# A branch hint ahead of the last branch, and loads moved from SyncE's queue to GpSimd's, in an attention and MLP kernel

## The chip, the cores and the metric

The kernel runs on one core of one Trainium2 chip. The metric is the device time of one execution in microseconds, the median of several runs. A profiled execution also gives a span, which is the time from the first to the last instruction of the program. Engines are named as in the profile: PE (TensorE matmul; PEld its weight loads), DVE (VectorE), ACT (ScalarE), POOL (GpSimd) and SP (SyncE). A q behind a name means the engine's sequencer, which handles waits, branches, register moves and DMA issues.

## What is computed

Eight batches of 12 heads, 448 positions and 64 channels go through attention with normalised queries and keys, and the result through a layer norm and a two-layer MLP with a residual:

```python
q_n, k_n = rmsnorm(q, g_q), rmsnorm(k, g_k)
scores = (q_n @ k_n.T) / sqrt(64)
attn = softmax(scores)                       # per head
x = heads_to_columns(attn @ v)               # 8 x 448 x 768
xn = (x - mean(x)) / sqrt(var(x) + 1e-6) * g_ln
out = x + maximum(xn @ w_ch1, 0) @ w_ch2     # 768 -> 3072 -> 768
```

## The kernel before, in words

The program has two ways to compute this. The **fast path** (class `_Fast`) works with 16-bit matmuls and a softmax without a maximum, which holds only while some sums and scales stay in bounds. The **general path** (`_general`, L786 to L894) is a slow loop over the eight batches that computes everything again and is safe for any data. The fast path always runs; while it runs it counts on DVE whether all its numbers were in bounds, and writes a flag (`flag`, L757, called from `run_rest` at L739). At the end each engine loads the flag into a register (L935) and branches on it (L936): into the general path if the flag is set, past it if not. For the inputs here it is not set, so the general path is only jumped over. In the stream of instructions of each engine it stands between the branch and the end of the program, so its length is the length of the jump.

Behind the branch, on the way past the general path, each engine raises the semaphore counts that the general path would have raised (these instructions carry the branch's line, L936). Then comes the end of the program (these carry L963): SP waits, one after another, until all DMA counters and all engines have reached their final counts, then two barriers over all engines follow, with a reset of the semaphores between them. The program also begins with a barrier over all engines (L952), which POOL gathers and releases.

Work of the fast path is cut into 25 **units** (`UNITS`, L23), each of one or two pairs of heads of one batch. `load_unit` (L168) brings a unit's k, q and v, for each of them a main part over 128 partitions (`load_main`, L125) and a rest in two halves (`load_left`, L131). Units up to 10 are loaded on SP's queue, later ones on POOL's (L171). Unit tiles come from a pool of two buffers, so unit 10's load goes into the buffer that unit 8 had. `pieces` (L189) prepares a unit: squares and sums for the norm, k times the two gains (`kg`, L225, on POOL at L229), the split of k into high and low halves, q scaled (L68), copies of v (L285, L291), and transposes by DMA on SP (L258 to L271) for later units. The order of work on PE, ACT, POOL and SP is written out by hand: by the list `ORDER` for the start, then by `attention` (L487), which gives each step of a unit a place among the scores and values of earlier pairs, and by `run_rest` (L729), which lays these steps between chunks of the MLP of the batch before. On DVE the scheduler sets the order.

`run_rest` walks over the batches. The last batch has no attention beside it any more: its MLP chunks (`mlp_chunks`, L641) run alone, 24 of the first layer (L652) and then those of the second (L668); DVE adds the residual (L672), and `store` (L704) issues the output on SP (L709) and, for the last 64 rows, on SP and ACT (L712). The normalised input of each MLP is transposed by DMA on SP (L624).

SP's and ACT's DMAs take eight semaphores in turn as counters, POOL's eight others.

The general path before has its 36 loads (L799) and its store (L893) on SP; each needs an address that depends on the loop's counter, which uses registers of the issuing engine.

Of the kernel before, what the change touches and what calls it, by code (L numbers as in the profile page):

```python
# [14 lines left out]
ENG = mybir.EngineType  # L15
# [61 lines left out]
class _Fast:  # L77
# [88 lines left out]
                                 for x in t]  # L166

    def load_unit(self, u):  # L168
        b, hs, m = UNITS[u]
        t = self.p_in.tile([128, 3, 14, D], FP32, tag="qkv", name="qkv")  # L170
        eng = self.nc.sync if u < 11 else self.nc.gpsimd  # L171
        for n in (1, 0, 2):
            self.load_main(eng, n, t[:, n, 0:6 * m], b, hs, 2 * m)
            self.load_left(eng, n, t[:, n, 6 * m:7 * m], b, hs, 2 * m)
        self.loads[u] = [t[:, n] for n in range(3)]

# [539 lines left out]
    def upto(self, target):  # L716
        while self.pos < min(target, len(self.steps)):
            for call in self.steps[self.pos]:
                call()
            self.pos += 1  # L720
# [8 lines left out]
    def run_rest(self):  # L729
        steps, mark, upto = self.steps, self.mark, self.upto  # L730
        tail = 13
        for b in range(B):
            chunks = list(self.mlp_chunks(b))
            total = sum(c for c, _ in chunks)
            if b + 1 == B:
                for i, (_, emit) in enumerate(chunks):
                    emit()
                    if i == 2:
                        self.flag()  # L739
                break  # L740
            start, goal = self.pos, mark[b + 1]
            done, items = 0.0, None
            for i, (cost, emit) in enumerate(chunks):
                if items and len(chunks) - i <= len(items):
                    items.pop(0)()
                emit()
                done += cost
                upto(int(min(goal, start + (goal - start) * done / (total - 960 * tail))))
                if self.pos >= goal and items is None:
                    items = self.ln_list(b + 1)  # L750
                    items.pop(0)()
            for op in items:
                op()
            if b + 2 == B:
                upto(len(steps))
# [30 lines left out]
def _general(tc, sh, q, k, v, g_q, g_k, out):  # L786

    nc = tc.nc
    P1, NS = 112, 4
    with ExitStack() as ctx:  # L790
# [4 lines left out]
        with tc.For_i(0, B) as b:  # L795
            for h in range(H):
                qkv = sb.tile([P1, 3, NS, D], FP32, tag="qkv", name="qkv")
                for n, src in enumerate((q, k, v)):
                    nc.sync.dma_start(  # L799
                        qkv[:, n].rearrange("p s d -> p (s d)"),  # L800
                        src[bass.ds(b, 1), h].rearrange("o (p s) d -> p (o s d)", p=P1))
                sq = sb.tile([P1, 2, NS, D], FP32, tag="sq", name="sq")
# [7 lines left out]
                for e in range(2):  # L810
# [3 lines left out]
                    out=kg, in0=qkv[:, 1],  # L814
# [70 lines left out]
            for s in range(NS):  # L885
                for g in range(2):
                    pC = ps.tile([P1, 384], FP32, tag="pC", name="pC")
                    for f in range(NFF):
# [1 line left out]
                                         start=(f == 0), stop=(f == NFF - 1))  # L890
                    nc.vector.tensor_tensor(out=x[:, s, ts(g, 384)], in0=pC,
                                            in1=x[:, s, ts(g, 384)], op=ALU.add)
            nc.sync.dma_start(out[bass.ds(b, 1)].rearrange("o (p s) d -> p (o s d)", p=P1),  # L893
                              x.rearrange("p s d -> p (s d)"))  # L894


@with_exitstack
def kernel(
    ctx: ExitStack,
    tc: tile.TileContext,  # L900
    q: bass.AP,
    k: bass.AP,
    v: bass.AP,
    g_q: bass.AP,
    g_k: bass.AP,
    moe_g_ln: bass.AP,
    moe_w_ch1: bass.AP,
    moe_w_ch2: bass.AP,
    out: bass.AP,
):  # L910
    nc = tc.nc
    sh = _Shared()
    const = ctx.enter_context(tc.tile_pool(name="const", bufs=1))
    sh.id16 = const.tile([128, 128], FP16, name="id16")
    make_identity(nc, sh.id16)
    sh.ones = const.tile([128, 1], FP32, name="ones")
    nc.vector.memset(sh.ones, 1.0)
    sh.warm = const.tile([128, 1], FP32, name="warm")
    sh.w2 = const.tile([128, NFF, DM], FP16, name="w2")
    sh.gg = sh.w2[:, 0, 0:4 * D].bitcast(FP32).rearrange("p (n d) -> p n d", n=2)  # L920
    sh.gprod = const.tile([128, D], FP32, name="gprod")
    sh.gmax = const.tile([128, 1], FP32, name="gmax")
    sh.gln = const.tile([128, DM], FP32, name="gln")
    sh.flag = const.tile([1, 1], INT32, name="flag")
    sh.w1 = const.tile([128, NDC, FF], FP16, name="w1")

    with ExitStack() as fctx:
        manual = {ENG.PE, ENG.Activation, ENG.Pool, ENG.SP}
        with tc.manual_schedule(engines=manual | {ENG.DVE}):
            fast = _Fast(fctx, tc, sh, q, k, v, (g_q, g_k), moe_g_ln, moe_w_ch1, moe_w_ch2, out)  # L930
            fast.run_first()
        with tc.manual_schedule(engines=manual):
            fast.run_rest()

    val = nc.values_load(sh.flag[0:1, 0:1], min_val=0, max_val=1)  # L935
    with tc.If(val > 0):  # L936
        _general(tc, sh, q, k, v, g_q, g_k, out)


# [28 lines left out]
```

## Time and profile before

| what | value |
|---|---|
| time before, median of 3 runs | 607.65 us |
| lowest and highest run | 606.86 and 607.78 us |
| time of the profiled execution | 606.57 us |
| its span | 604.8 us |
| PE busy in the span | 575.8 us (95%) |
| DVE, ACT, POOL busy | 287.3, 358.4, 184.0 us |

A row of the profile that stands for one line reads: line, engine, operation, tile, count, then durations in ns (least, median, most), then the starts of the first and of the last in microseconds of the span. A row of the timeline begins with start and length in microseconds; what stands in brackets is the idle time before it and what ended it. "DMA to landing" is the time from a transfer's issue to its count on its semaphore. The page's DMA queues give the packets, the megabytes and a share of time; the queues of kind "instruction" carry the program's own code.

### The profile page before, as it was taken

The numbers are of one execution on the slowest core, as the hardware profiler recorded it, in microseconds if no ns is written. First come the engines' busy times: TensorE is split into PE (matmuls) and PEld (weight loads), VectorE is DVE, ScalarE is ACT, GpSimd is POOL, SyncE is SP. The second block draws the span as 40 slices with busy tenths as digits, with TensorE's granted clock in tenths as the row PEclk, the third lists the DMA queues.
The fourth block names the chain that finished last, engine by engine and source line by source line (L and its number), as shares of the span: only waits on it lengthen the run. The fifth ranks groups of instructions, "written<-read, shape, count | busy, mean of one in ns | idle before, by whom it ended". The sixth has DMA issues, their size and how long they took to land.

```text
span 604.8 us, 11485 instructions
## 1 busy us (share of the span) xinstructions
PE 575.8 (95%) x4500; PEld 340.3 (56%) x4500; DVE 287.3 (48%) x643; ACT 358.4 (59%) x673; POOL 184.0 (30%) x245
## 2 busy tenths in 40 slices
PE   2887999999999999999999999999999999999995
PEld 1555666655565666654566666654566666654564
DVE  5899567734356256714256255734256322530011
ACT  5996887368843697448754498538755387124200
POOL 2853432233541355332542345424412000000000
PEclk9999999999999999999999999999999999999999
DMA  8998999484966487948856486948724330130011
GB/s 229 272 198 198 218 226 190 94 175 122 150 140 133 106 111 158 179 123 97 130 140 125 96 118 156 191 114 124 140 58 84 79 62 1 37 95 0 1 53 57
DMA packets 130861, 75.29 MB, mean 124 GB/s; under 512 B 96656, under 2 KB 121040, under 8 KB 130800
## 3 DMA queue, kind: packets, MB, share of 16 engines
q1 hardware_dynamic: 114048, 45.12, 38.4%
q0 software_dynamic: 16080, 28.94, 22.5%
q8 instruction: 37, 0.61, 0.4%
q10 hardware_dynamic: 672, 0.43, 0.2%
q14 instruction: 24, 0.20, 0.1%
HBM read 52.36 MB, written 11.01 MB: 105 GB/s over the span
## 4 chain that ended last, share of the span: by engine, by line
PE 88%; ACT 2%; DVE 2%; issue 0%; DVEq 0%
PE psC L668 36%; PE psH L652 35%; PE psS L353 8%; PE oA L408 5%; PE oB L410 2%; PE psS L359 1%; ACT E L371 1%; PE tr L316 0%; ACT khl L215 0%; PE psU L698 0%; DVE stat L576 0%; ACT hT L654 0%; PE tr L330 0%; DVE xn L597 0%; DVE x L425 0%
## 5 line engine op out<-in xcount | busy, mean ns | idle before, releaser
L652 PE MATMUL psH<-xnT,w 128*128 128x512 f16 (+1 forms) x1134 | 242.0, 353 | 0.0
L668 PE MATMUL psC<-w,hT 128*128 128x384 f16 (+1 forms) x1368 | 234.8, 323 | 0.0
L371 ACT ACTIVATE E<-psS,rr_all 128x448 f16<-128x448 f32 x312 | 193.4, 635 | 48.7 <-PE psS L353 47.8
L654 ACT ACTIVATE hT<-psH 128x512 f16<-128x512 f32 (+1 forms) x189 | 104.0, 550 | 132.2 <-PE psH L652 130.9
L668 PEld LDWEIGHTS <-hT 128*128 128x128 f16 x1368 | 127.2, 98 | 78.8 <-issue 4.3
L652 PEld LDWEIGHTS <-w 128*128 128x128 f16 x1134 | 102.4, 98 | 83.3 <-issue 2.9
L353 PE MATMUL psS<-qU,kU 128*128 128x448 f16 x288 | 101.0, 357 | 8.6 <-ACT E L371 5.7
L408 PEld LDWEIGHTS <-E 128*128 128x128 f16 x936 | 64.5, 98 | 44.5 <-issue 5.1
L229 POOL TENSOR_TENSOR qkv<-qkv,gprod 128x896 f32<-128x896 f32 x21 | 43.6, 2078 | 92.5 <-ACT khl L215 41.1
L408 PE MATMUL oA<-v,E 128*128 128x65 f16 x864 | 66.6, 194 | 0.1
L672 DVE SCALAR_TENSOR_TENSOR x<-psC,rs_all,x 128x384 f32<-128x384 f32 x48 | 29.2, 616 | 78.5 <-PE psC L668 78.1
L128 POOL DMA_DIRECT2D qkv<-in_k_dram x14 | 11.2, 796 | 137.7 <-ACT E L371 82.5
L410 PE MATMUL oB<-v,E 128*128 128x65 f16 x288 | 51.9, 194 | 0.1
L423 DVE RECIPROCAL rec_all<-oA 128x6 f32<-128x6 f32 x48 | 9.3, 194 | 88.1 <-PE oA L408 87.6
L218 DVE TENSOR_REDUCE ssq<-khl 128x14 f32<-128x896 f32 (+1 forms) x24 | 25.6, 1065 | 44.6 <-ACT khl L215 44.5
L353 PEld LDWEIGHTS <-kU 128*128 128x128 f16 x288 | 28.1, 98 | 25.7 <-issue 5.8
L218 DVE TENSOR_REDUCE ssq<-qn 128x14 f32<-128x896 f32 (+1 forms) x25 | 26.1, 1046 | 21.9 <-ACT qn L215 21.8
L68 DVE SCALAR_TENSOR_TENSOR qn<-qkv,rr_all 128x256 f16<-128x256 f32 (+1 forms) x72 | 26.4, 425 | 18.1 <-ACT rr_all L222 18.1
L410 PEld LDWEIGHTS <-E 128*128 128x128 f16 x312 | 30.2, 97 | 0.2 <-DVE xl L430 0.2
L425 DVE TENSOR_TENSOR x<-oA,rec_all 128x384 f32<-128x384 f32 x48 | 26.8, 558 | 1.5
L576 DVE BATCH_NORM_STATS2 stat<-x 128x6 f32<-128x256 f32 (+1 forms) x75 | 26.0, 404 | 0.6
L240 DVE TENSOR_TENSOR khl<-qkv,khl 128x896 f16<-128x896 f32 x21 | 22.7, 1079 | 4.0 <-ACT khl L237 3.9
(111 smaller groups left out, 443.1 us busy)
## 6 DMA issues: line engine op xcount, KB each, us to landing
out_dram<-x SPq DMA_DIRECT2D x20, 384.0 KB, 2.5
qkv<-in_k_dram POOLq DMA_DIRECT2D x14, 384.0 KB, 3.8
qkv<-in_q_dram POOLq DMA_DIRECT2D x14, 384.0 KB, 5.5
qkv<-in_v_dram POOLq DMA_DIRECT2D x14, 384.0 KB, 7.2
w<-in_moe_w_ch_dram POOLq DMA_DIRECT2D x3, 1536.0 KB, 13.0
w<-in_moe_w_ch_dram POOLq DMA_DIRECT2D x2, 2304.0 KB, 22.8
qkv<-in_k_dram SPq DMA_DIRECT2D x7, 384.0 KB, 6.1
qkv<-in_q_dram SPq DMA_DIRECT2D x7, 384.0 KB, 5.7
```

What stands on the lines that cost most here:

```text
L68: nc.vector.scalar_tensor_tensor(out=out, in0=x, scalar=8.0, in1=r.unsqueeze(2).broadcast_to([x.shape[0], g, D]), op0=ALU.mult, op1=ALU.mult)
L218: nc.vector.tensor_reduce(out=c["ssq"][:, n], in_=c["sq", n], axis=AX.X, op=ALU.add)
L229: (nc.vector if u in DVE_KG else nc.gpsimd).tensor_tensor(out=c["t"][1], in0=c["t"][1], in1=sh.gprod.unsqueeze(1).broadcast_to([128, g, D] ...
L353: nc.tensor.matmul(ps[0][:, 0:S], c["main"][:, ts(i, 128)], c["q"][:, ts(h, S)], start=True, stop=True)
L371: nc.scalar.activation(out=o, in_=x[:, 0:S], func=AFT.Exp, scale=self.units[u][3][:, g:g + 1], bias=EXP_BIAS)
L408: nc.tensor.matmul(oA[:, t, cs], E[:, ts(t, 128)], rhs, start=(i == 0 and t == 0), stop=(i == 6 and t == 2))
L410: nc.tensor.matmul(oB[:, cs], E[:, 320:448], rhs, start=(i == 0), stop=(i == 6))
L425: nc.vector.tensor_tensor(out=x[:, :, 128 * hp:128 * hp + 128].rearrange("p t (e d) -> p t e d", e=2), in0=oA[:, :, :, 0:D], in1=rec[:, 0: ...
L652: nc.tensor.matmul(ps[:, 0:N], sh.w1[:, dc, ts(f, 128)], xnT[:, dc, 0:N], start=(dc == 0), stop=(dc == NDC - 1))
L654: nc.scalar.activation(out=hT[:, f, 0:N], in_=ps[:, 0:N], func=AFT.Relu)
L668: nc.tensor.matmul(ps[:, 0:g[1]], hT[:, f, ts(t, 128)], sh.w2[:, f, cols], start=(f == 0), stop=(f == NFF - 1))
L672: nc.vector.scalar_tensor_tensor(out=x[:, cols], in0=ps[:, 0:g[1]], scalar=self.rs[:, b, t:t + 1], in1=x[:, cols], op0=ALU.mult, op1=ALU.add)
```

## The change

There are three edits. The branch gets the label "general", and `run_rest` marks, 40 chunks ahead of the end of the last batch's MLP, a place for a hint on all five engines that this branch is likely taken. The general path's loads and its store are issued by POOL in place of SP. And of unit 10's six DMA groups one, the main part of v, is issued by POOL in place of SP.

```diff
     def load_unit(self, u):
+        nc = self.nc
         b, hs, m = UNITS[u]
         t = self.p_in.tile([128, 3, 14, D], FP32, tag="qkv", name="qkv")
         eng = self.nc.sync if u < 11 else self.nc.gpsimd
         for n in (1, 0, 2):
-            self.load_main(eng, n, t[:, n, 0:6 * m], b, hs, 2 * m)
+            self.load_main(nc.gpsimd if u == 10 and n == 2 else eng, n, t[:, n, 0:6 * m], b, hs, 2 * m)
             self.load_left(eng, n, t[:, n, 6 * m:7 * m], b, hs, 2 * m)
...
             if b + 1 == B:
                 for i, (_, emit) in enumerate(chunks):
+                    if i == len(chunks) - 40:
+                        self.tc.mark_branch_hint_location("general", "LikelyTaken", [ENG.PE, ENG.DVE, ENG.SP, ENG.Activation, ENG.Pool])
                     emit()
...
                 for n, src in enumerate((q, k, v)):
-                    nc.sync.dma_start(
+                    nc.gpsimd.dma_start(
                         qkv[:, n].rearrange("p s d -> p (s d)"),
...
-            nc.sync.dma_start(out[bass.ds(b, 1)].rearrange("o (p s) d -> p (o s d)", p=P1),
+            nc.gpsimd.dma_start(out[bass.ds(b, 1)].rearrange("o (p s) d -> p (o s d)", p=P1),
                               x.rearrange("p s d -> p (s d)"))
...
-    with tc.If(val > 0):
+    with tc.If(val > 0, label="general"):
         _general(tc, sh, q, k, v, g_q, g_k, out)
```

The edits add three lines, so lines of the changed kernel behind them are numbered one to three higher: the branch is L939 there, the reading of the flag L938, the end of the program L966.

## The prediction

> **What bounds the kernel now.** I read the page first (shares and the 40 slices), then the waits of TensorE, then the chain that ended last, then, line by line, the last eight microseconds.
>
> ```profile
> span 604.8 us, 11485 instructions
> PE 575.8 (95%) x4500; PEld 340.3 (56%) x4500; DVE 287.3 (48%) x643; ACT 358.4 (59%) x673; POOL 184.0 (30%) x245
> PE   2887999999999999999999999999999999999995
> ```
> TensorE is busy in nearly every slice but the first five (some 75 us) and the last. Its waits from 80 us on are one row:
>
> ```profile
> PE psS L353 <- ACT E L371: 0.4, 2, 0.2
> ```
> So from 80 us on nothing outside TensorE makes time or loses it, until its last matmul. The chain from 590 us shows where that is:
>
> ```profile
> 589.90 8.52 PE psC L668 x76
> 598.43 0.02 issue
> 598.45 0.42 DVE xl L672
> ```
> Compute ends at 598.9 us, and the span at 604.8: 5.9 us in which no engine computes. Those are the stage of this change. The views of L712 (the last stores, from 598.5 us), L935 (each engine reads the flag), L936 (the branch, and what stands first behind it) and L963 (the closing waits and barriers) show it; the times are first and last starts.
>
> ```profile
> L712 SPq DMA_DIRECT2D out_dram<-xl x1: 466/466/466, 598.9 to 598.9; - x1
> L712 ACTq DMA_DIRECT2D out_dram<-xl x1: 498/498/498, 598.9 to 598.9; - x1
> DMA to landing us min/median/max: 2.2/2.7/3.1
> ```
> ```profile
> L935 PEldq TENSOR_LOAD <-flag x1: 488/488/488, 596.8 to 596.8; - x1
> L935 DVEq TENSOR_LOAD <-flag x1: 539/539/539, 598.5 to 598.5; - x1
> L935 ACTq TENSOR_LOAD <-flag x1: 959/959/959, 599.4 to 599.4; - x1
> ```
> ```profile
> L936 SPq EVENT_SEMAPHORE  x8: 17/17/17, 602.6 to 603.1; - x8
> L936 POOLq COMPARE_BRANCH  x1: 53/53/53, 540.6 to 540.6; - x1
> L936 PEldq COMPARE_BRANCH  x1: 4102/4102/4102, 597.4 to 597.4; - x1
> L936 DVEq COMPARE_BRANCH  x1: 72/72/72, 599.1 to 599.1; - x1
> L936 SPq COMPARE_BRANCH  x1: 58/58/58, 599.4 to 599.4; - x1
> L936 ACTq COMPARE_BRANCH  x1: 54/54/54, 600.5 to 600.5; - x1
> L936 ACTq EVENT_SEMAPHORE  x1: 17/17/17, 601.0 to 601.0; - x1
> L936 PEldq EVENT_SEMAPHORE  x1: 51/51/51, 601.5 to 601.5; - x1
> L936 DVEq EVENT_SEMAPHORE  x1: 21/21/21, 602.4 to 602.4; - x1
> ```
> ```profile
> L963 SPq EVENT_SEMAPHORE  x12: 27/28/28, 603.2 to 603.8; - x12
> ```
> Read it engine by engine. From branch to next instruction SP takes 3.2 us (599.4 to 602.6), DVE 3.3 (599.1 to 602.4), PE 4.1 inside the branch's own record, ACT 0.5 (600.5 to 601.0). DVE, PE and ACT wait there for nothing but their own finished work. So on three engines the branch itself stalls. The page's instruction queues say with what:
>
> ```profile
> q8 instruction: 37, 0.61, 0.4%
> q14 instruction: 24, 0.20, 0.1%
> ```
> Code is loaded in pieces, 0.61 MB in 37 packets (16 KB) and 0.20 MB in 24 (8 KB). In the built program the general path lies between branch and end: 156 instructions on SP, 438 on DVE, 1809 on PE, 141 on ACT, 26 on POOL. The one that jumps 141 pays 0.5 us, those that jump 156 and more pay over 3: the target's code isn't there and has to be fetched.
>
> SP sets the end. Once its code is there it passes 20 waits in a row, 8 of L936 and 12 of L963, 602.6 to 603.8, none of them held up (0.06 to 0.07 us each, their spacing); from the start of the last one to the end of the span it is 1.0 us (603.8 to 604.8: drains, two barriers).
>
> **The change, part by part.** General path: 36 loads and a store go from SP's code to POOL's. By the built programs SP then jumps 37 instructions, POOL 139; and the 8 waits of L936 leave SP, POOL getting 4 and one count-up instead. DVE, PE and ACT jump as far as before. For SP the new jump is shorter than ACT's, which paid 0.5 us, and longer than POOL's 26, so I price it at ACT's 0.5: SP's first closing wait starts at 599.9 in place of 603.2. POOL's longer jump, even if it stalled 3.3 us like DVE's, is at 540.6 us, and POOL is needed again only in the closing barriers, behind SP's last wait: 60 us of cover. With less cover than 3.3 us it would cost the difference.
>
> What is late next? SP's 12 waits must see, in program order, the DMA lanes and then DVE's, PE's and ACT's work past their branches. With SP alone mended, DVE is last (602.4): SP passes its count in the tenth wait and two more behind it, the twelfth starting at 602.6. Before it started at 603.8. That is worth 1.2 us.
>
> The hint: the built program has a branch hint on all five engines. It stands not 40 chunks from the end but as the first instruction on PE, DVE, ACT and SP and ahead of the first of POOL's kernel instructions, some 600 us before the branch, with no other branch in between. Which way is "taken"? The trace says that the way past the general path is the one that costs a far jump, so that is the one that a hint can help. No row shows a hint's work, so it is bounded: nothing (DVE and PE stall as before), or the whole stall down to ACT's 0.5 us (DVE at 599.6, PE at 597.9). I take the second: a hint names its branch, the code of the end has to come in only once, and both engines stand near the branch long before it (PE's last 76 matmuls alone take 8.5 us, twice its stall, and DVE follows them).
>
> [...]
>
> With SP, DVE and PE free, ACT (601.0) and the last two stores remain. The stores are issued at 598.9; over the whole run L712 reads:
>
> ```profile
> DMA to landing us min/median/max: 1.9/2.2/3.1
> ```
> At the median they have landed at 601.1 (bounds: the least here and the most of the last pair, 600.8 and 602.0). DMAs of SP and ACT take eight counters in turn, and there are now 296 of them in place of 297: the last two stores hold the last two counters that SP looks at, and one wait or none lies behind. So the twelfth starts at 601.2 in place of 603.8. Gain: **2.6 us**, with bounds 1.7 and 2.8.
>
> Costs at the start. The register moves for the general path's addresses go from SP to POOL, ahead of POOL's drain, for which all engines wait at 0.5 us:
>
> ```profile
> L952 SPq MOVE  x4: 29/34/42, 0.0 to 0.2; - x4
> L952 POOLq EVENT_SEMAPHORE  x2: 17/17/17, 0.5 to 0.6; - x2
> L952 SPq DRAIN  x1: 7/7/7, 0.3 to 0.3; - x1
> ```
> SP was ready at 0.3 and not the last, so its relief is worth nothing; four moves spaced 0.06 make POOL, which was last, 0.2 us later. A hint costs each engine what a short sequencer instruction does, 0.02 (the waits) to 0.07 (the branches): 0.1 at most, on all engines beside each other. TensorE waits in its first slices, so both go through to the end: **0.3 us**, bounds 0 and 0.4.
>
> Unit 10: the load of v, 128 partitions, goes from SP to POOL. On POOL it stands behind unit 9's L229 and ahead of its casts:
>
> ```profile
> 99.15 1.29 DVE L68 SCALAR_TENSOR_TENSOR qn<-qkv,rr_all 128x256 f16<-128x256 f32 x4
> 108.61 2.08 POOL L229 TENSOR_TENSOR qkv<-qkv,gprod 128x896 f32<-128x896 f32 x1 [12.78 <-DMA qU<-qn]
> 110.64 0.83 POOL L285 CAST v<-qkv 128x768 f16<-128x768 f32 x1
> 111.40 0.64 POOL L291 CAST vl<-qkv 64x128 f16<-64x128 f32 x2
> 130.15 0.80 POOL L128 DMA_DIRECT2D qkv<-in_k_dram  x1 [18.11 <-ACT E L371]
> L128 POOL DMA_DIRECT2D qkv<-in_v_dram x14: 782/784/792, 134.1 to 430.6; - x14
> 127.52 0.60 SPq L128 DMA_DIRECT2D qkv<-in_v_dram  x1
> 129.52 2.15 SPq L258 DMA_TRANSPOSE kU<-khl  x1
> L624 SPq DMA_TRANSPOSE xnT<-xn x4: 1215/1234/1237, 113.6 to 117.6; - x4
> DMA to landing us min/median/max: 2.7/2.8/2.8
> L652 PE MATMUL psH<-xnT,w x12: 379/379/379, 122.4 to 124.9; 128*128 128x512 f16 x12
> ```
> It waits for unit 8's last reader on DVE (the first row, done at 100.4), so it issues at 110.7 and takes 0.78; the casts come 0.8 later, and POOL then has 18.1 us of idle time to take that up. SP's transposes of unit 9 come up to 0.6 earlier. The transfer moves from 127.5 to 110.7, and may meet the four xnT transposes, the last issued at 117.6 and landed 2.8 us later (the row under theirs) at 120.4; TensorE wants xnT at 122.4. Cover 2.0 us, past that one for one. With TensorE never waiting there: **0**, bounds 0 and 1.
>
> **Sum.** 2.6 - 0.3 = 2.3 us. The profiled execution took 606.57 us, 1.77 outside its span; it would take 604.3, with a span of 602.5. It lies 1.08 below the median of the runs, and since none of the terms scales with that, I take the 2.3 from the median: 607.65 - 2.3 = **605.35 us**.
>
> **Rivals.**
> [...]
> *PE alone pays*: its next instruction at 601.5 goes through SP's last two waits; the twelfth starts at 601.6, gain 2.2 - 0.3 = 1.9: 605.75.
> [...]
>
> **How the numbers follow.** Forecast 0.62, PE alone 0.08, not heeded 0.18, not heeded and SP stalling 0.04, slower 0.08. About 0.2% (1.2 us) is what a measurement of this kernel can tell from no change. Faster by more (under 606.4): 0.62 + 0.08 = 0.70. Within: 0.18 + 0.04 = 0.22. Slower: 0.08. The range takes in the forecast's bounds (1.7 - 0.4 to 2.8 - 0, so 604.85 to 606.35), some way below for the spread of the three runs (606.86 to 607.78), and above up to the unheeded hint: 604.4 to 606.9.
>
> **What would show it.** In the changed kernel's profile: DVE's and PE's L939 instruction behind the branch within 0.5 us (forecast) or over 3 (not heeded); SP's closing waits starting at about 599.9 and one of the last two ending at a landing; a start 0.2 to 0.3 us later; POOL with a 0.78 us load at about 111 and TensorE without new waits behind 80 us. I am wrong if TensorE's last matmul moves by over half a microsecond, if DVE's stall stays, or if the landing slips towards 602.

## The result, and the profile after

The changed kernel takes **604.52 us** (median of 7 runs, 604.02 to 605.83) against 607.65 us (606.86 to 607.84). The ratio is 0.9961 with a 95% interval of 0.9951 to 0.997, that is 2.4 us less (1.8 to 3.0). The profiled execution took 604.02 us with a span of 602.5 us.

From its page first the span, the busy times and TensorE's row of the 40 slices:

```profile
span 602.5 us, 11487 instructions
PE 575.8 (96%) x4500; PEld 340.0 (56%) x4500; DVE 287.3 (48%) x643; ACT 358.5 (60%) x673; POOL 184.8 (31%) x246
PE   2787999999999999999999999999999999999997
```
And the row of TensorE's waits on ScalarE's exponentials, from 80 us on:

```profile
PE psS L354 <- ACT E L372: 0.4, 2, 0.2
```
TensorE does the same work and waits as little. The last slice of its row has gone from 5 to 7: the same tail end of matmuls stands in a shorter remainder. The chain from 588 us says where compute ends now:

```profile
587.96 10.80 PE psC L669 x90
598.76 0.02 issue
598.79 0.42 DVE xl L673
```
That is 599.2 us, 0.3 later than before. From there to the end of the span it is 3.3 us, where it was 5.9 (604.8 - 598.9). This stretch, from DVE's last operation to the end, is called the tail below. The whole gain is in it. The branch's line, in the view that showed it before (the columns are again durations in ns and first and last start in us):

```profile
L939 POOLq COMPARE_BRANCH  x1: 63/63/63, 541.0 to 541.0; - x1
L939 PEldq COMPARE_BRANCH  x1: 393/393/393, 597.7 to 597.7; - x1
L939 PEldq EVENT_SEMAPHORE  x1: 51/51/51, 598.8 to 598.8; - x1
L939 DVEq COMPARE_BRANCH  x1: 84/84/84, 599.4 to 599.4; - x1
L939 SPq COMPARE_BRANCH  x1: 78/78/78, 599.7 to 599.7; - x1
L939 DVEq EVENT_SEMAPHORE  x1: 21/21/21, 600.0 to 600.0; - x1
L939 ACTq COMPARE_BRANCH  x1: 72/72/72, 600.8 to 600.8; - x1
L939 ACTq EVENT_SEMAPHORE  x1: 17/17/17, 601.3 to 601.3; - x1
```
DVE goes from its branch to the next instruction in 0.6 us (it was 3.3). PE's branch takes 0.39 us (it was 4.10), and its next instruction, which waits for PE's last matmul, follows at 598.8, when that is done (587.96 + 10.80 in the chain). SP's own view, the closing waits, is next (twelve of them; the thirteenth instruction, of 17 ns at 601.8, belongs to the barrier behind them):

```profile
L966 SPq EVENT_SEMAPHORE  x13: 17/28/328, 600.0 to 601.8; - x13
```
The same view cut to what starts from 600.95 us on:

```profile
L966 SPq EVENT_SEMAPHORE  x2: 28/28/28, 601.5 to 601.5; - x2
```
And the issues of the last two stores, with the time from issue to landing of the stores there:

```profile
L713 SPq DMA_DIRECT2D out_dram<-xl x1: 466/466/466, 599.2 to 599.2; - x1
L713 ACTq DMA_DIRECT2D out_dram<-xl x1: 498/498/498, 599.2 to 599.2; - x1
...
DMA to landing us min/median/max: 2.0/2.1/2.2
```
SP starts its closing waits at 600.0 instead of 603.2. Ten of the twelve are through by 600.95 (one of them holds SP for 328 ns); the last two both start at 601.5, which is when the later of the last two stores (ACT's, 2.2 us to landing; SP's took 2.0), issued at 599.2, has landed. So a store's landing now ends the kernel, where before it was SP's late arrival at a list of waits that were all met. It does so by little: the last wait also needs ACT, which is past its branch only at 601.3, so an earlier landing would have gained no more than about 0.1 us.

The start: three rows of the program's first microsecond, from the views of L955 (the first barrier) and L966 (the hints carry the line of the program's end), then the load of unit 10 in GpSimd's timeline (start and duration in us). Both stand where they were forecast:

```profile
L955 POOLq MOVE  x4: 29/29/39, 0.2 to 0.4; - x4
L955 POOLq EVENT_SEMAPHORE  x2: 17/17/17, 0.8 to 0.8; - x2
L966 SPq BRANCH_PREFETCH_HINT  x1: 56/56/56, 1.0 to 1.0; - x1
```
```profile
109.28 2.08 POOL L230 TENSOR_TENSOR qkv<-qkv,gprod 128x896 f32<-128x896 f32 x1 [13.13 <-DMA qU<-qn]
111.30 0.80 POOL L128 DMA_DIRECT2D qkv<-in_v_dram  x1
112.10 0.84 POOL L286 CAST v<-qkv 128x768 f16<-128x768 f32 x1
```
The first barrier is gathered at 0.8 instead of 0.5 us. The four hints other than SP's took 50 to 60 ns each.

### The profile page after: what moved, and what is told of

Its sections match the earlier page's. It is cut to its first block, busy times and chain, and to the rows that moved or that the text cites. A ratio compares the mean times of both kernels' runs of the same rounds, so it can differ in the third digit from the quotient of the medians.

```text
span 602.5 us, 11487 instructions
## 1 busy us (share of the span) xinstructions
PE 575.8 (96%) x4500; PEld 340.0 (56%) x4500; DVE 287.3 (48%) x643; ACT 358.5 (60%) x673; POOL 184.8 (31%) x246
## 4 chain that ended last, share of the span: by engine, by line
PE 86%; DVE 3%; ACT 2%; DMA 1%; issue 1%; SPq 0%; DVEq 0%; ACTq 0%
PE psH L653 35%; PE psC L669 34%; PE psS L354 7%; PE oA L409 5%; PE oB L411 2%; PE psS L360 1%; DMA kU<-khl 1%; ACT E L372 1%; DVE stat L577 1%; ACT khl L216 1%; PE psU L699 0%; DVE x L426 0%; DVE ssq L219 0%; ACT hT L655 0%; DVE khl L241 0%
```

## The experiments

The theory to be tested, inferred from the gaps of 3.2 to 4.1 us behind the branches before: a jump to code that isn't at hand stalls an engine for its fetch; the queue moves make SP's jump short; the hint brings DVE's and PE's target in ahead; SP's last closing wait sets the end, whichever engine or store it is that holds it. The rivals are that the moves alone do it, or that one part of the hint alone does.

The profiles' spans can't be set beside each other as they are: compute ended anywhere from 598.9 to 600.7 us in them. So the tail is read from each, and the time from the ratios. Each tail is a difference of two rounded times and good to about 0.1 us. Each ratio is to the kernel before on the same chip; runs 1 to 4 shared a chip, and so did runs 5 to 8.

| run | jumps past the general path | span - end of DVE = tail, us | ratio (95%) |
|---|---|---|---|
| before | SP, DVE, PE stall | 604.8 - 598.9 = 5.9 | 1 |
| whole change | none stalls | 602.5 - 599.2 = 3.3 | 0.9961 (0.9951 to 0.997) |
| 1 moves alone | DVE, PE stall | 604.4 - 599.6 = 4.8 | 0.9977 (0.9968 to 0.9985) |
| 2 hint alone | none stalls | 603.8 - 599.6 = 4.2 | 0.9979 (0.9971 to 0.9988) |
| 3 hint on PE and DVE, no moves | SP stalls | 605.6 - 599.6 = 6.0 | 1.0003 (0.9994 to 1.0012) |
| 4 moves, hint on DVE | PE stalls | 603.7 - 600.3 = 3.4 | 0.9968 (0.9955 to 0.9981) |
| 5 moves, hint on PE | DVE stalls | 605.6 - 600.7 = 4.9 | 0.9984 (0.9973 to 0.9994) |
| 6 moves, hint on PE and DVE | none stalls | 602.8 - 599.2 = 3.6 | 0.9966 (0.9952 to 0.9979) |
| 7 whole change but unit 10 | none stalls | 604.1 - 600.7 = 3.4 | 0.9963 (0.995 to 0.9977) |
| 8 whole change again | none stalls | 603.3 - 600.0 = 3.3 | 0.9963 (0.9951 to 0.9974) |

### 1: the moves alone

```diff
-                    if i == len(chunks) - 40:
-                        self.tc.mark_branch_hint_location("general", "LikelyTaken", [ENG.PE, ENG.DVE, ENG.SP, ENG.Activation, ENG.Pool])
```


> The queue moves alone, no hint on any engine. Theory (a jump to code that is not at hand stalls for its fetch; the moves shorten SP's jump, the hint brings DVE's and PE's target in ahead; SP's last closing wait sets the end): SP passes its branch within 0.5 us, DVE still takes 3.3 us and PE 4.1, DVE is last at about 602.7 of the span, gain 0.9 us, ratio to before 0.9985. Rival (the moves do it all and the hint is decoration): ratio 0.996, DVE and PE through their branches in under 1 us. Start 0.2 us later than before, as with the whole change, by both.

Measured: 605.63 us against 607.13, tail 4.8. Its branch line and SP's closing waits:

```profile
L937 PEldq COMPARE_BRANCH  x1: 4322/4322/4322, 598.1 to 598.1; - x1
L937 DVEq COMPARE_BRANCH  x1: 72/72/72, 599.8 to 599.8; - x1
L937 SPq COMPARE_BRANCH  x1: 58/58/58, 600.2 to 600.2; - x1
L937 DVEq EVENT_SEMAPHORE  x1: 21/21/21, 603.3 to 603.3; - x1
```
```profile
L964 SPq EVENT_SEMAPHORE  x12: 28/28/2048, 600.4 to 603.4; - x12
```
SP is through its jump in 0.2 us, without any hint. DVE takes 3.5 us and PE 4.3, and one of SP's waits holds it for 2.05 us, until DVE is there. The tail is 1.1 us shorter than before; less 0.2 at the start that is the 0.9 expected, at the edge of what the ratio allows (0.9 to 1.9 us). The rival that the moves do it all falls by the two stalls: they are still there.

### 2: the hint alone

The kernel before, with the label and the mark of the hint:

```diff
+                    if i == len(chunks) - 40:
+                        self.tc.mark_branch_hint_location("general", "LikelyTaken", [ENG.PE, ENG.DVE, ENG.SP, ENG.Activation, ENG.Pool])
...
-    with tc.If(val > 0):
+    with tc.If(val > 0, label="general"):
```


> The hint on all five engines alone; loads and stores stay on SP. Theory: SP, DVE and PE all pass their branches within 0.6 us though SP still jumps over 156 instructions; but SP has its 8 + 12 waits, the first held by a store that lands at about 601.2, so that its last wait starts at about 602.4 in place of 603.8: gain 1.4 us less 0.1 for the hints, 1.3, ratio 0.9978. No 0.2 us at the start. Rival (the moves do it all): SP still 3.2 us behind its branch, ratio 1.000.

Measured: 605.92 us against 607.13, tail 4.2. SP in its two stretches of waits:

```profile
L938 SPq EVENT_SEMAPHORE  x8: 17/17/17, 601.5 to 602.1; - x8
L938 SPq COMPARE_BRANCH  x1: 78/78/78, 600.1 to 600.1; - x1
```
```profile
L965 SPq EVENT_SEMAPHORE  x12: 28/28/28, 602.1 to 602.8; - x12
```
With the hint SP's gap is shorter as well, over the 156 instructions that the prediction counted: its next instruction starts 1.4 us behind the branch (3.2 before). That is also 1.9 us behind the issue of SP's own last store at 599.6, for whose landing it was expected to wait (SP's last store took 2.0 us with the whole change), so how much of the 1.4 us is the jump doesn't show. But 8 + 12 waits are still to come, and they take the 1.3 us from 601.5 to 602.8. The tail is 1.7 us shorter, less 0.1 for the hints 1.6; the ratio says 1.3 (0.7 to 1.8). So hint and moves are each worth something by themselves, and both shorten SP's gap (3.2 us before) to 1.4 and 0.2. By the tails they are worth a little less together (2.6 us) than their sum (1.1 + 1.7); by the ratios (2.4 against 1.4 + 1.3, each good to about half a microsecond) that can't be told.

### 3: the hint on PE and DVE, without the moves

As run 2, with `[ENG.PE, ENG.DVE]` as the engines of the hint.

> The hint on PE and DVE alone; loads and stores stay on SP, and SP has no hint. Theory: DVE and PE pass in 0.6 us, but SP stalls 3.2 us and then has its 20 waits, all met: the end stays where it was, ratio 1.000 (0.9995 to 1.0005). Rival (PE's and DVE's stalls set the end, SP only waits for them): gain of 1 to 2 us, ratio 0.997 to 0.998.

Measured: 607.35 us against 607.13, tail 6.0.

```profile
L938 SPq EVENT_SEMAPHORE  x8: 17/17/17, 603.4 to 603.9; - x8
L938 PEldq COMPARE_BRANCH  x1: 393/393/393, 598.1 to 598.1; - x1
L938 SPq COMPARE_BRANCH  x1: 58/58/58, 600.2 to 600.2; - x1
L938 DVEq EVENT_SEMAPHORE  x1: 21/21/21, 600.4 to 600.4; - x1
```
DVE and PE are 3 us earlier than before and it is worth nothing, because SP still spends 3.2 us behind its branch (600.2 to 603.4). This is the cleanest test of "SP sets the end", and the rival falls.

### 4 and 5: the moves, and the hint on one engine

The whole change, with `[ENG.DVE]` and with `[ENG.PE]` as the engines of the hint.

> The whole change, but the hint on DVE alone. Theory: PE takes 4.1 us behind its branch, until about 601.8; SP's eleventh closing wait ends there and the twelfth starts at 601.9, 0.4 us later than with the whole change (601.5): span 602.9, ratio 0.9968. ACT, SP and POOL need no hint: ACT's next instruction again 0.5 us behind its branch. Rival (the hint matters on ACT or SP): ACT or SP stalls 3 us, span above 604.

> The whole change, but the hint on PE alone. Theory: PE passes in about 1 us, DVE stalls 3.3 us and is last, the same end as with the moves alone: SP's tenth closing wait held about 2 us, ratio 0.9985 (0.9977 was measured for the moves alone). Rival (a hint on any engine is enough, or DVE's jump got short by the moves): ratio 0.996.

Measured: 605.23 us against 607.13, tail 3.4, and 606.64 us against 607.49, tail 4.9. PE in run 4 and SP's last two closing waits there, then DVE in run 5:

```profile
L939 PEldq COMPARE_BRANCH  x1: 3758/3758/3758, 598.8 to 598.8; - x1
L939 PEldq EVENT_SEMAPHORE  x1: 51/51/51, 602.6 to 602.6; - x1
```
```profile
L966 SPq EVENT_SEMAPHORE  x2: 28/118/209, 602.5 to 602.7; - x2
```
```profile
L939 DVEq COMPARE_BRANCH  x1: 72/72/72, 600.9 to 600.9; - x1
L939 DVEq EVENT_SEMAPHORE  x1: 21/21/21, 604.4 to 604.4; - x1
```
Run 5 has the tail of run 1: once SP's jump is short, DVE's stall is nearly the whole of what the hint saves. Run 4 shows what PE's adds beyond that. PE reaches its branch 1.5 us before DVE's last operation ends (598.8 against 600.3), so most of its stall lies beside the landing of the last stores; the eleventh wait starts when ACT's store has landed (602.5) and then holds SP for another 0.2 us, until PE is there. The tail is only 0.1 us longer than with the whole change where 0.4 was expected, because the stall was 3.8 us in this profile and 4.1 had been put in; in run 1 it was 4.3, so this term varies with the stall.

### 6: the moves, and the hint on PE and DVE

The whole change, with `[ENG.PE, ENG.DVE]`.

> The whole change, but the hint on PE and DVE alone. Theory: the same end as with the whole change, since SP's jump is 37 instructions and ACT's 141 was cheap before; the first loads of SP and ACT go out 0.1 us earlier. Ratio 0.996, span 602.4 give or take the start. Rival (SP, ACT or POOL need the hint too): 3 us behind a branch of SP or ACT.

Measured: 604.77 us against 607.49, tail 3.6. No engine stalls (PE's branch takes 0.4 us, and SP, ACT and DVE go on 0.2, 0.5 and 0.6 us behind theirs); the tail is 0.3 longer than with the whole change because in this execution the last stores took longer:

```profile
DMA to landing us min/median/max: 2.4/2.5/2.5
```
The two kernels can't be told apart by time. The hints on SP, ACT and POOL were not needed once the moves were there.

### 7 and 8: without unit 10's load, and the whole change again

In run 7 `load_main` takes `eng` again for every load of unit 10; the rest of the change stays.

> The whole change without unit 10's load on GpSimd. Theory: 297 DMAs on the eight counters again, so that the last of SP's two stores sits on the counter that SP looks at fifth; its landing then holds that wait, and seven waits of 0.06 us come behind it: the twelfth starts 0.2 to 0.4 us later than with the whole change (601.5), if the front ends at the same time. Ratio 0.9965. Rival (that load matters for the body: transposes or casts): TensorE's last matmul moves by over 0.5 us, or new waits of TensorE behind 80 us.

> The whole change once more, beside the three others on one chip: ratio 0.9961 as in the result, 0.9951 to 0.997.

Measured: 604.99 and 604.95 us against 607.49, tails 3.4 and 3.3. Run 7's closing waits, and then those of them from 602.6 us on:

```profile
L966 SPq EVENT_SEMAPHORE  x12: 27/28/28, 601.5 to 603.2; - x12
```
```profile
L966 SPq EVENT_SEMAPHORE  x8: 27/28/28, 602.7 to 603.2; - x8
```
SP passes four waits from 601.5 on, stands at the fifth until 602.7 (SP's last store was issued at 600.75), and has eight starts from there on, 0.06 us apart. With the whole change it stood at the eleventh. Measured from the end of DVE's last operation the twelfth starts 2.4 us later here (603.15 - 600.73) and 2.3 us later there (601.5 - 599.2): the order is worth 0.1 us, where 0.2 to 0.4 was expected, because there the held wait is ACT's store, which landed a little later than SP's. Time doesn't show it. TensorE's last matmul did end 1.5 us later in this profile than in that of the whole change, and the rival named just that as its sign. But with the edit in place compute ended just as late in run 5 (600.7), and the whole change's own executions have spans from 602.5 to 604.2 us, a scatter as wide as this difference. In runs 5 and 7 the granted clock was also the lowest of all the profiles (0.995 and 0.996, against 0.999 and 1.000). TensorE's waits from 80 us on are 0.7 us here and 0.4 with the whole change, but 0.8 in run 5, which has the edit. So nothing here can be put down to unit 10.

## Why the prediction was right, point by point

- **The sum: right.** Forecast were 605.35 us, a gain of 2.3; measured were 604.52 and, by the ratio, a gain of 2.4 (1.8 to 3.0). The 2.6 us forecast for the tail are what the two profiles show (5.9 to 3.3). That the median lies 0.8 us below the forecast is partly chance: the seven runs lie in two groups, 604.02 to 604.52 and 605.39 to 605.83, and the median is the highest of the lower one.
- **What bounds it: right.** The body didn't change, and the tail did. Of the tail, SP's arrival at its closing waits was the bound (run 3). Two small misreadings cost nothing: TensorE's row is below 9 in its first four slices, not five, and the first of SP's 20 waits follow each other by 0.08 to 0.10 us, not by 0.06 to 0.07 (the end of the list was read off, not added up).
- **SP's short jump: right, priced too high.** 0.5 us was taken from ACT; SP took 0.2 (run 1: 600.2 to 600.4). Nothing hung on it, since the waits were held later anyway. POOL's longer jump took 0.5 us even without a hint (run 1: 541.4 to 541.9) and had the cover that was counted on.
- **DVE next, 0.9 us for SP alone: right.** Runs 1 and 5 have tails 1.1 and 1.0 us shorter, less 0.2 at the start.
- **The hint is heeded from the first instruction on: right.** It executed at 1.0 us, and the branches that it names ran at 597.7 to 600.8 us. With the hint DVE's jump (438 instructions by the prediction's count) takes 0.6 us and PE's (1809) takes 0.4, without it 3.3 to 3.5 and 3.8 to 4.3. That the stalls are waits for code is the author's explanation of 3.2 us on SP (before and run 3), 3.3 to 3.5 on DVE (before, runs 1 and 5) and 3.8 to 4.3 on PE (before, runs 1 and 4). The instruction queues agree with it, no more: from 590 us on they moved 8 packets before (6 on q14, 2 on q8) and 3 after (2 and 1). Which engine a packet was for isn't shown, nor when a hinted target's code came in; that it has to come in only once was the author's estimate.
- **The landing ends the kernel: right, its size partly by luck.** Forecast was 2.2 us from issue to landing, the median of the whole run; no reason was given why the last pair, which had taken 2.2 to 3.1 before, should come down to it, and at 3.1 the gain from the tail would have been 1.7 instead of 2.6. It was 2.2 for the later store, and the twelfth wait started at 601.5, the forecast's 601.2 and the 0.3 by which everything comes later. The landing got shorter with the change, 2.2 us for the later store instead of 3.1. The last pair in run 1 and then in run 5, where DVE stalls, reads

  ```profile
  DMA to landing us min/median/max: 2.5/2.8/3.1
  ```
  ```profile
  DMA to landing us min/median/max: 2.1/2.6/3.2
  ```

  The later store takes 3.1 to 3.2 us in the three profiles in which DVE stalls (before, runs 1 and 5), and 2.2 to 2.5 in three in which it doesn't (the whole change, runs 6 and 8). So the shorter landing goes along with the hint on DVE; how the two hang together isn't shown.
- **0.3 us at the start: right in place, not shown at the end.** The gathering moved from 0.5 to 0.8 us, and the hints come on top. Compute ended 0.3 later too, but between profiles it scatters by 1.8 us (598.9 to 600.7), far more than that, so whether the 0.3 arrives is open.
- **Unit 10: right.** The load issued at 111.3 and took 0.80; the casts came behind it; TensorE's waits stayed at 0.4 us.
- **Rivals.** A hint that isn't heeded would have left SP's short jump alone, a gain of 1.2 - 0.3 = 0.9 us, so 606.75 (0.9985 of before); run 1, which has no hint, measured 0.9977 (0.9968 to 0.9985), and the whole change lies well below that. "PE alone" was mis-sized: 0.4 us were forecast for PE's stall and the tail of run 4 shows 0.1, with a stall of 3.8 us where 4.1 was put in. The slower outcome didn't happen. The DMA queues of the changed kernel in its first 25 us have no instruction queue among them, so nothing was fetched at once for the hint at 1.0 us:

  ```profile
  q1 hardware_dynamic: 9228, 5.75, 80.5%
  q0 software_dynamic: 160, 0.23, 6.9%
  q10 hardware_dynamic: 432, 0.23, 3.0%
  ```

## What to carry to other kernels

Rare code at the end of a program still has to be jumped over, and here a far jump cost 3.2 to 4.3 us on each of SP, DVE and PE while it had neither a hint nor a short way; look at the gap between the branch and the next instruction of each engine, not at the time to the last compute. Shortening the jump (fewer instructions of the rare path on that engine) and announcing the branch both shortened SP's gap here (from 3.2 us to 0.2 and 1.4, with tails of 4.8 and 4.2 instead of 5.9), and without one of them on SP, the engine that closes this program, the hint on PE and DVE was worth nothing (run 3, 6.0). When such a stall goes, look at the list of closing waits: the last-landing store is best looked at last, though here that is worth 0.1 us at most, too little for the time to show.

## What the runs showed of the hardware

- With a hint some 600 us ahead of its branch (1.0 against 597.7 to 600.8 us), on PE with 4500 matmuls and as many weight loads in between, the jump took 0.4 us on PE and 0.6 us on DVE, against 4.1 and 3.3 before.
- The page's instruction queues, after, read

```profile
q8 instruction: 36, 0.59, 0.4%
q14 instruction: 21, 0.17, 0.1%
```

  against 37 and 24 packets before: one packet of some 16 KB (0.59 MB / 36) and three of some 8 KB (0.17 MB / 21) fewer.
- The hints show no packet on q8 in addition to the others. From 590 us on q8 reads, in run 1 (no hint) and then in run 5 (the hint on PE alone),

  ```profile
  q8 instruction: 2, 0.03, 0.9%
  ```
  ```profile
  q8 instruction: 1, 0.02, 0.4%
  ```

  and before and after likewise 2 and 1 packets. With 37 and 36 on the pages before and after that leaves 35 ahead of 590 us in both. Whether one of these 35 brought PE's target, and in place of what, isn't shown.
- The branch's own record was longer with the hint on DVE (84 instead of 72 ns), SP (78 instead of 58), ACT (72 or 73 instead of 54) and POOL (63 instead of 53).
- A jump without a stall isn't free: 0.5 us on ACT in every run, 0.6 on DVE with the hint, 0.2 to 0.3 on SP with the moves (run 1 and the whole change).
